# Attention values share a pair of PSUM banks with the next group's scores, transposes go in pairs, and weight rounding moves inside MLP 2's gate

## The chip, the core and the metric

One Trainium2 (trn2) chip, one of its cores. The metric is device microseconds (us) of one execution. The engines are TensorE (PE; its weight loads are listed as PEld), VectorE (DVE), ScalarE (ACT), GpSimd (POOL) and SyncE (SP, which here only issues DMA transfers). Each engine works through its own instructions in the order written; semaphores join them.

## What is computed

Local attention over chunks of 32 queries, with 8 memory keys in front of each window, then two MLPs one after the other, all in fp32 with 3072 tokens (4 x 768) of width 512 and a hidden width of 2048.

```python
for c in range(24):                       # per batch and head (8 heads of 64)
    k_full = concat([mem_k, k[c*32 - 16 : c*32 + 32 + 8]])
    scores = q_c @ k_full.T / 8
    a = exp(scores - max(scores)); a = a / (sum(a) + 1e-9)
    out[c] = a @ v_full
x = out                                   # 3072 x 512
h = x @ w1_in;  x = (h - tanh(h)) @ w1_out
h = x @ w2_in
g = h if h >= 1, 0 if h <= -1, else (h + 1)**2 / 4
out = g @ w2_out
```

The weights arrive as 64-bit floats and are rounded to fp32 on the chip.

## The kernel before

**Tiles.** A group `t` is four chunks (128 tokens) of all eight heads; there are 24 groups. A block `b` is four groups (512 tokens); there are 6. The MLPs run in 192 steps `s`: MLP 1 (`phase` 0) has 6 blocks of 16 slices `fc` of 128 hidden units, then MLP 2 (`phase` 1) the same. An fp32 product is made of three products of rounded halves: `hi*hi`, `hi*lo` and `lo*hi` (tiles `whi`, `wlo`, `xh`, `xl`, `ghi`, `glo`). So `hidden(s)` and `output(s)` are 12 matmuls of 128x512 each.

**The main loop.** Iteration `i` (called step `i` below) issues, in this order: the split of the weights of later slices (`whi` on ACT, then `wlo` on DVE), `gate_end(i)`, the split of the gate of `output(i-15)`, the events of the table `before`, `hidden(i+1)`, `gate(i+1)`, the events of the table `behind`, and `output(i-16)`. Outputs run 16 steps behind the hidden products, so block 0 of MLP 1 (steps 0 to 15) has no outputs to compute. The hidden product goes to PSUM tile `h`, of which there are two.

**The gate.** In MLP 1 it is a tanh on ACT (L371) and a subtraction on DVE (L372). In MLP 2 DVE clamps `h` (L374), ACT squares (L377), and `gate_end`, one step later, takes the larger of that and `h` on DVE (L382), which also frees `h`:

```python
gate_end(i)                 # at the start of step i: DVE, L382
...
run events "before"         # rounding of one weight slice: ACT L119, L122; DVE L128, L129, L137; L142
hidden(i + 1)
gate(i + 1)                 # DVE L374, ACT L377
```

**Rounding of weights** (`round_weights`): two ACT passes, three DVE passes and one addition (L142), on POOL for MLP 1's weights and on DVE for MLP 2's. It runs at steps 0 to 27 for MLP 1 and at steps 79 to 121 for MLP 2, one slice in most of these steps.

**Attention.** Groups 0 to 3 run ahead of the loop. The others are spread over the loop through `behind`, in four parts, one part to a step, a group to every 3.4 steps in block 0 and to every 4 later: part 0 scores (32 small fp32 matmuls on 64 rows by 32 columns of the array, 64 instructions in the trace, into two PSUM banks `s`), maximum, subtraction and exp; part 1 sum and four transposes `t`, copied to `at`; part 2 values (as many small matmuls, into two banks `v`) and normalisation `xn`; part 3 four transposes `x`, split into `xh` (ACT) and `xl` (DVE, L307), which are the next block's input. All of these take banks from one pool `ps_a` of two.

Of the kernel before, what the change touches and what calls it, by code (L numbers as in the profile page):

```python
# [55 lines left out]
ATT1 = (1, 3.4)  # L56
# [9 lines left out]
def tile_memory_attention_two_mlps(  # L66
# [24 lines left out]
    ps_a = ctx.enter_context(tc.tile_pool(name="ps_a", bufs=2, space=PSUM))  # L91
# [52 lines left out]
    def round_weights(phase, which, fc):  # L144
        round_act(phase, which, fc)
        round_mag(phase, which, fc)
        round_sign(phase, which, fc)
# [21 lines left out]
    def att_load(t):  # L169
        if t >= NG:  # L170
            return
        q = att.tile([128, NQ], F32, tag="q", name=f"q{t}")
        k = att.tile([128, NK], F32, tag="k", name=f"k{t}")
        v = att.tile([128, NV], F32, tag="v", name=f"v{t}")
        att_dma(t, q, (k[:, :NK // 2], k[:, NK // 2:]), (v[:, :NV // 2], v[:, NV // 2:]))
# [3 lines left out]
    def att_load_start(t):  # L179
# [6 lines left out]
        att_dma(t, q, (k0, k1), (v0, v1), True)  # L186

    def att_dma(t, q, k, v, weights=False):
        q = q.rearrange("p (j a c) -> p j a c", j=GC, a=NPAIR)
        k = [x.rearrange("p (j a c) -> p j a c", j=2, a=NPAIR) for x in k]  # L190
        v = [x.rearrange("p (j c) -> p j c", j=2) for x in v]
# [8 lines left out]
        if weights:  # L200
            load_weights(0, 0, t)

        for i in range(2):
# [6 lines left out]
        st[t] = {  # L210
            "q": [q[:, j] for j in range(GC)],
            "k": [k[j // 2][:, j % 2] for j in range(GC)],
            "v": [v[j // 2][:, j % 2] for j in range(GC)],
        }
# [3 lines left out]
    def att_scores(t, ps):  # L218
        qt, kt = st[t]["q"], st[t]["k"]
        sp = [ps(f"s{t}_{hh}") for hh in range(2)]  # L220
        for pr in range(NPAIR):
            for j in range(GC):
                for hh in range(2):
                    nc.tensor.matmul(  # L224
                        sp[hh][j * CHUNK:(j + 1) * CHUNK, pr * WIN:(pr + 1) * WIN],
# [6 lines left out]
    def att_exp(t):  # L232

        e = att.tile([128, 4, 2, WIN], F32, tag="e", name=f"e{t}")
        mx = att.tile([128, H], F32, tag="mx", name=f"mx{t}")
        for hh in range(2):
            s = st[t]["sp"][hh][:, :NPAIR * WIN].rearrange("p (a k) -> p a k", a=NPAIR)

            if t % GPB == 0:
                nc.vector.memset(s[:CHUNK, :, NMEM:NMEM + LEFT], NEG)  # L240
            if t % GPB == GPB - 1:
                nc.vector.memset(s[128 - CHUNK:, :, WIN - SEEN:], NEG)
            m = mx[:, hh * NPAIR:(hh + 1) * NPAIR]
            nc.vector.tensor_reduce(out=m, in_=s, op=ALU.max, axis=AX.X)
            nc.vector.tensor_tensor(  # L245
                out=e.rearrange("p (b c) u k -> p c u b k", c=2)[:, hh],
                in0=s.rearrange("p (u b) k -> p u b k", u=2),
                in1=m.rearrange("p (u b) -> p u b", u=2)[:, :, :, None].to_broadcast([128, 2, 2, WIN]),
                op=ALU.subtract,
            )  # L250
        nc.scalar.activation(out=e, in_=e, func=AF.Exp, scale=scale)  # L251
        st[t]["e"] = e
# [8 lines left out]
    def att_transpose(t, ps):  # L261
        p = ps(f"t{t}")
        e = st[t]["e"].rearrange("p g u k -> p g (u k)")
        for g in range(4):
            nc.tensor.transpose(p[:, g * GQ:(g + 1) * GQ], e[:, g, :], ident)  # L265
        at = att.tile([128, 4, GQ], F32, tag="at", name=f"at{t}")
        nc.scalar.activation(out=at, in_=p.rearrange("p (g c) -> p g c", g=4), func=AF.Copy)
        st[t]["at"] = at

    def att_values(t, ps):  # L270
        at, v = st[t]["at"], st[t]["v"]
        vp = [ps(f"v{t}_{u}") for u in range(2)]
        for g in range(4):
            for j in range(GC):
                for u in range(2):
                    nc.tensor.matmul(  # L276
                        vp[u][j * CHUNK:(j + 1) * CHUNK, g * D:(g + 1) * D],
# [6 lines left out]
    def att_norm(t):  # L284
        vp, r = st[t]["vp"], st[t]["r"]
        xn = att.tile([128, 2, 4, D], F32, tag="xn", name=f"xn{t}", bufs=1)
        for u in range(2):
            nc.vector.tensor_tensor(
                out=xn[:, u], in0=vp[u][:, :4 * D].rearrange("p (g d) -> p g d", g=4),
                in1=r[:, :, u][:, :, None].to_broadcast([128, 4, D]), op=ALU.mult,  # L290
# [296 lines left out]
```

## Time and profile before

| | us |
|---|---|
| median of 3 runs | 1192.4 (1191.47 to 1192.63) |
| the profiled execution, whole | 1190.61 |
| its span (first to last instruction) | 1188.8 |
| PE busy | 1148.5 (97%) |
| DVE busy | 788.5 (66%) |
| ACT busy | 589.0 (50%) |
| POOL busy | 42.5 (4%) |

The span runs from the first instruction to the last; the whole time holds 1.8 us more, around it. PE is busy nearly all the time, so what counts is where it is not, and how much of its busy time is small matmuls and transposes.

### The profile page before, as it was taken

Reading aid. Unit: us, or ns where it says so; the run is one execution under the profiler, and the core shown is the slowest. Engines: PE = TensorE matmul, PEld = TensorE weight load, DVE = VectorE, ACT = ScalarE, POOL = GpSimd, SP = SyncE. Lnnn points to the kernel's source line nnn. Section 1 sums busy time; section 2 is a strip of 40 time slices with the busy share of each in tenths; the row PEclk is TensorE's granted clock in tenths of the full one; section 3 lists DMA queues with packets and bytes.
Section 4 is the critical chain, followed back from the end, with each engine's and each line's share of the span. In section 5 each row is a group of like instructions: output and inputs, shape, how many; then the busy total and the mean of one; then the engine's idle time right before and its main releaser. Section 6 shows DMA issues by size and latency. Waiting matters only on the chain.

```text
span 1188.8 us, 19761 instructions
## 1 busy us (share of the span) xinstructions
PE 1148.5 (97%) x7931; PEld 923.3 (78%) x7931; DVE 788.5 (66%) x1394; ACT 589.0 (50%) x1018; POOL 42.5 (4%) x38
## 2 busy tenths in 40 slices
PE   7888999999999999999999988999999999999998
PEld 3566888888888888888887766788888888888886
DVE  5689886655655565588877777766666666665653
ACT  3456664444444454466655455454445454544443
POOL 1223221000000000000000000000000000000000
PEclk9989999999999999999999999999999999999999
DMA  9777552222221143032232122010010000000000
GB/s 230 204 200 203 150 143 63 81 60 57 81 64 45 45 107 125 2 107 107 71 107 89 55 87 89 1 71 1 1 72 1 1 36 1 1 36 1 1 36 36
DMA packets 94268, 85.18 MB, mean 72 GB/s; under 512 B 54496, under 2 KB 79072, under 8 KB 93408
## 3 DMA queue, kind: packets, MB, share of 16 engines
q1 hardware_dynamic: 94176, 83.91, 23.9%
q8 instruction: 63, 1.03, 0.4%
q14 instruction: 29, 0.24, 0.1%
HBM read 71.30 MB, written 12.58 MB: 71 GB/s over the span
## 4 chain that ended last, share of the span: by engine, by line
PE 80%; DVE 12%; ACT 3%; issue 3%; DMA 0%; SPq 0%; ACTq 0%; DVEq 0%
PE acc L407 39%; PE h L359 37%; DVE wlo L162 2%; PE v L276 2%; ACT g L377 2%; DVE g L382 2%; PE s L224 1%; DVE g L374 1%; DVE raw L137 1%; DVE glo L389 1%; ACT whi L155 1%; DVE raw L142 1%; PE t L265 1%; DVE raw L129 1%; PE x L300 1%
## 5 line engine op out<-in xcount | busy, mean ns | idle before, releaser
L162 DVE TENSOR_TENSOR wlo<-raw,whi 128x512 fp32r<-128x512 f32 x384 | 265.1, 690 | 152.4 <-ACT whi L155 152.4
L155 ACT ACTIVATE whi<-raw 128x512 fp32r<-128x512 f32 x384 | 240.0, 625 | 32.2 <-PE acc L407 31.2
L359 PE MATMUL h<-xh,whi 128*128 128x512 f32 x768 | 209.5, 395 | 14.2 <-DVE g L382 13.0
L407 PE MATMUL acc<-ghi,whi 128*128 128x512 f32 x768 | 219.0, 399 | 1.9 <-DVE y L420 1.7
L407 PE MATMUL acc<-ghi,wlo 128*128 128x512 f32 x768 | 211.8, 390 | 0.0
L407 PE MATMUL acc<-glo,whi 128*128 128x512 f32 x768 | 211.4, 389 | 0.0
L359 PE MATMUL h<-xl,whi 128*128 128x512 f32 x768 | 207.4, 392 | 1.1 <-DVE xl L307 1.1
L359 PE MATMUL h<-xh,wlo 128*128 128x512 f32 x768 | 206.8, 391 | 0.0
L377 ACT ACTIVATE g<-g,half 128x512 f32<-128x512 f32 x96 | 69.4, 723 | 265.6 <-DVE g L374 265.6
L359 PEld LDWEIGHTS h<-xh,whi 128*128 128x128 f32 x768 | 142.2, 188 | 49.8 <-ACT whi L155 19.1
L389 DVE TENSOR_TENSOR glo<-g,ghi 128x512 fp32r<-128x512 f32 x192 | 131.7, 686 | 62.4 <-PE acc L407 61.3
L359 PEld LDWEIGHTS h<-xl,whi 128*128 128x128 f32 x768 | 145.2, 189 | 32.2 <-DVE xl L307 1.6
L359 PEld LDWEIGHTS h<-xh,wlo 128*128 128x128 f32 x768 | 145.3, 189 | 30.6
L407 PEld LDWEIGHTS acc<-ghi,wlo 128*128 128x128 f32 x768 | 144.2, 188 | 31.0
L407 PEld LDWEIGHTS acc<-glo,whi 128*128 128x128 f32 x768 | 144.2, 188 | 30.6
L407 PEld LDWEIGHTS acc<-ghi,whi 128*128 128x128 f32 x768 | 139.6, 188 | 31.5 <-issue 2.1
L388 ACT ACTIVATE ghi<-g 128x512 fp32r<-128x512 f32 x192 | 119.9, 624 | 73.7 <-PE acc L407 73.6
L372 DVE TENSOR_TENSOR g<-h,g 128x512 f32<-128x512 f32 x96 | 66.2, 689 | 96.4 <-ACT g L371 96.0
L371 ACT ACTIVATE g<-h 128x512 f32<-128x512 f32 x96 | 57.2, 596 | 128.7 <-PE h L359 126.8
L374 DVE TENSOR_SCALAR g<-h 128x512 f32<-128x512 f32 x96 | 66.1, 689 | 42.8 <-PE h L359 42.6
L382 DVE TENSOR_TENSOR g<-h,g 128x512 f32<-128x512 f32 x96 | 65.7, 684 | 1.7 <-ACT g L377 1.7
L251 ACT ACTIVATE e<-e 128x512 f32<-128x512 f32 x24 | 15.2, 632 | 73.8 <-DVE e L245 73.8
(50 smaller groups left out, 599.7 us busy)
## 6 DMA issues: line engine op xcount, KB each, us to landing
stage<-w_in SPq DMA_DIRECT2D x32, 512.0 KB, 4.1
stage<-w_out SPq DMA_DIRECT2D x32, 512.0 KB, 3.4
k<-qkv_t SPq DMA_DIRECT2D x80, 128.0 KB, 4.1
v<-qkv_t SPq DMA_DIRECT2D x80, 128.0 KB, 3.2
yd<-y SPq DMA_DIRECT2D x24, 256.0 KB, 2.7
yin<-yd SPq DMA_DIRECT2D x6, 1024.0 KB, 5.5
out_t<-y SPq DMA_DIRECT2D x24, 256.0 KB, 2.1
q<-qkv_t SPq DMA_DIRECT2D x20, 256.0 KB, 3.9
```

Of the source, the lines that this page charges most:

```text
L155: nc.scalar.activation(out=hi, in_=r, func=AF.Copy)
L162: nc.vector.tensor_tensor(out=lo, in0=r, in1=hi.bitcast(F32), op=ALU.subtract)
L276: nc.tensor.matmul(vp[u][j * CHUNK:(j + 1) * CHUNK, g * D:(g + 1) * D], at[u * WIN:(u + 1) * WIN, g, j * CHUNK:(j + 1) * CHUNK], v[j][u * ...
L359: nc.tensor.matmul(hp, w[:, kc * 128:(kc + 1) * 128], x[:, kc, :], start=j == 0 and kc == 0, stop=j == 2 and kc == KC - 1,)
L371: nc.scalar.activation(out=g, in_=hp, func=AF.Tanh)
L372: nc.vector.tensor_tensor(out=g, in0=hp, in1=g, op=ALU.subtract)
L374: nc.vector.tensor_scalar(out=g, in0=hp, scalar1=-1.0, scalar2=1.0, op0=ALU.max, op1=ALU.min)
L377: nc.scalar.activation(out=g, in_=g, func=AF.Square, scale=0.5, bias=half)
L382: nc.vector.tensor_tensor(out=g_t[s], in0=hp, in1=g_t[s], op=ALU.max)
L388: nc.scalar.activation(out=hi, in_=g, func=AF.Copy)
L389: nc.vector.tensor_tensor(out=lo, in0=g, in1=hi.bitcast(F32), op=ALU.subtract)
L407: nc.tensor.matmul(acc_t[dm][:, :n], w[:, dm * 128:(dm + 1) * 128], g, start=fc == 0 and j == 0, stop=fc == FC - 1 and j == 2,)
```

## The change

- Attention of group `t` is issued in three slots: `slot_a` at step `i`, `slot_exp` at `i+1`, `slot_b` at `i+2`. Groups start every 3 steps for groups 4 to 8 and every 4 from there; group 4 starts at step 0 (before: step 1).
- `slot_a(t)` issues the values of group `t-1` and the scores of group `t` back to back. Both lie in one PSUM tile of two banks, values in the first half of each bank, scores in the second. Behind them come the normalisation of `t-1` and the maximum and subtraction of `t`. The maximum and the normalisation are one DVE instruction each (before: two).
- `slot_exp(t)` issues the exp and the sum, one step later than the maximum.
- `slot_b(t)` issues the transposes `x` of group `t-1` and `t` of group `t` back to back, into another such tile. The pool `ps_a` holds one tile of two banks, so a slot waits until the slot before it has been read.
- Keys and queries of group `t+2` are loaded at step `i+1`, values of `t+1` too; before, all of group `t+2` at part 3.
- In MLP 2 the three DVE passes and the addition of the rounding stand between the clamp and the maximum of the gate, and the maximum (`gate_end`) moves to the step of its clamp. In MLP 1 the rounding keeps its place.
- The output accumulators are two tiles of two banks (before: four of one).

```diff
-ATT1 = (1, 3.4)
+SPACE_A = (3, 4)
...
-    ps_a = ctx.enter_context(tc.tile_pool(name="ps_a", bufs=2, space=PSUM))
+    ps_a = ctx.enter_context(tc.tile_pool(name="ps_a", bufs=1, space=PSUM))
...
-    def att_scores(t, ps):
+    def att_scores(t, pair):
-        sp = [ps(f"s{t}_{hh}") for hh in range(2)]
+        sp = pair[:, :, 4 * D:].rearrange("p c (a k) -> p c a k", a=NPAIR)
...
-    def att_values(t, ps):
+    def att_values(t, pair):
-        vp = [ps(f"v{t}_{u}") for u in range(2)]
+        vp = pair[:, :, :4 * D].rearrange("p u (g d) -> p u g d", g=4)
...
+    def slot_a(t):
+        pair = ps_a.tile([128, 2, 512], F32, tag="a", name=f"a{t}")
+        if t - 1 >= PER:
+            att_values(t - 1, pair)
+        if t < NG:
+            att_scores(t, pair)
+        if t - 1 >= PER:
+            att_norm(t - 1)
+        if t < NG:
+            att_max(t)
+
+    def slot_exp(t):
+        att_exp(t)
+        att_sum(t)
+
+    def slot_b(t):
+        pair = ps_a.tile([128, 2, 512], F32, tag="a", name=f"b{t}")
+        if t - 1 >= PER:
+            att_x(t - 1, pair[:, 0, :])
+        if t < NG:
+            att_transpose(t, pair[:, 1, :])
+        if t - 1 >= PER:
+            att_xh(t - 1)
+        if t < NG:
+            att_at(t)
+        if t - 1 >= PER:
+            att_xl(t - 1)
...
-    for t in range(PER, NG):
-        b, k = t // PER - 1, t % PER
-        i = ATT1[0] + ATT1[1] * k if b == 0 else FC * b - 1 + 4 * k
-        for part in range(4):
-            at_step(behind, i + part, att_part, t, part)
-        if t + 2 < NG:
-            at_step(before, i + 3.01, att_load, t + 2)
-    at_step(before, 1.5, att_load, PER + 1)
+    for t in range(PER, NG + 1):
+        k = t - PER
+        i = SPACE_A[0] * min(k, PER) + SPACE_A[1] * max(0, k - PER)
+        at_step(behind, i, slot_a, t)
+        if t < NG:
+            at_step(behind, i + 1, slot_exp, t)
+        at_step(behind, i + 2, slot_b, t)
+        at_step(before, i + 1.01, att_load, t + 2, True, False)
+        if t - 1 >= PER:
+            at_step(before, i + 1.02, att_load, t + 1, False, True)
+    at_step(before, 0.5, att_load, PER + 1)
...
-                    at_step(before, p, round_weights, phase, w, fc)
+                    at_step(before, p, round_act, phase, w, fc)
+                    at_step(rounds, p, round_rest, phase, w, fc)
...
-        if 0 <= i < NS:
-            gate_end(i)
...
+        run(before, i)
+        second = i + 1 < NS and steps[i + 1][0] == 1
+        if not second:
+            run(rounds, i)
         if i + 1 < NS:
             hidden(i + 1)
             gate(i + 1)
+        if second:
+            run(rounds, i)
+        if i + 1 < NS:
+            gate_end(i + 1)
+        run(behind, i)
         if o >= 0:
             output(o)
```

**PE, block 1 of MLP 1.** The order of PE's instructions around groups 8 and 9 before the change. `h17` is the hidden product of step 17, `acc` the output accumulators, `v8`, `t8` and `x8` the values and transposes of group 8; the 32 matmuls of the values alternate between `v8_0` and `v8_1`.

```order
L265 MATMUL t8_1689<-ident_99,e8_1641 128x128 x4
L407 MATMUL acc0_0_1696<-ghi0_1574,whi1_0_1578 128x512
...
L359 MATMUL h18_1733<-xh_0_1_943,wlo0_18_1650 128x512 x4
L276 MATMUL v8_0_1749<-v8_1313,at8_1694 32x64
L276 MATMUL v8_1_1750<-v8_1313,at8_1694 32x64
...
L359 MATMUL h19_1831<-xh_0_1_943,wlo0_19_1714 128x512 x4
L300 MATMUL x8_1849<-ident_99,xn8_1783 128x128 x4
L407 MATMUL acc0_0_1696<-ghi2_1716,whi1_2_1720 128x512
```

The same place after the change; `a9` and `b9` are the shared tiles of the slots of group 9.

```order
L385 MATMUL h17_1638<-xh_0_1_1006,wlo0_17_1582 128x512 x4
L287 MATMUL a9_1654<-v8_1319,at8_1577 32x64 x32
L231 MATMUL a9_1654<-k9_1313,q9_1312 32x64 x32
L434 MATMUL acc0_0_1726<-ghi0_1584,whi1_0_1588 128x512 x2
...
L385 MATMUL h19_1827<-xh_0_1_1006,wlo0_19_1742 128x512 x4
L307 MATMUL b9_1843<-ident_99,xn8_1719 128x128 x4
L273 MATMUL b9_1843<-ident_99,e9_1721 128x128 x4
L434 MATMUL acc0_0_1726<-ghi2_1744,whi1_2_1748 128x512 x2
```

Four interruptions of the large matmuls for each group have become two.

**ACT, block 0.** ACT's order around the exp of group 5 before: `g5` is the tanh of step 5, `e5` the exp, `whi0_7` the split of a weight slice.

```order
L371 ACTIVATE g5_940<-h5_927 128x512
L302 ACTIVATE xh_0_1_943<-x4_945 128x4x128
L251 ACTIVATE e5_986<-e5_986 128x512
L155 ACTIVATE whi0_7_995<-raw00_7_840 128x512
L119 ACTIVATE raw00_9_999<-stage00_9_807 128x512
```

And after, from the step of the group's maximum on:

```order
L397 ACTIVATE g4_846<-h4_833 128x512
L154 ACTIVATE whi0_6_922<-raw00_6_788 128x512
L119 ACTIVATE raw00_8_926<-stage00_8_750 128x512
L122 ACTIVATE stage00_8_750<-stage00_8_750 128x512
L397 ACTIVATE g5_960<-h5_947 128x512
L261 ACTIVATE e5_916<-e5_916 128x512
L154 ACTIVATE whi0_7_968<-raw00_7_824 128x512
```

The subtraction that the exp needs is issued on DVE right behind `g4`'s, so a whole step of ACT's work now stands between the two.

**DVE, MLP 2.** DVE's order around the gate of step 112 before: `raw11_8` is the weight slice that is rounded, `y95` the copy of a finished output.

```order
L389 TENSOR_TENSOR glo96_7572<-g96_6820,ghi96_7571 128x512
L162 TENSOR_TENSOR wlo1_96_7577<-raw11_0_7050,whi1_96_7575 128x512
L128 TENSOR_SCALAR raw11_8_7581<-raw11_8_7581 128x512
L129 TENSOR_SCALAR raw11_8_7581<-raw11_8_7581 128x512
L137 SCALAR_TENSOR_TENSOR raw11_8_7581<-stage11_8_7438,raw11_8_7581 128x512
L142 ISA raw11_8_7581<-stage11_8_7438,raw11_8_7581 128x1024
L374 TENSOR_SCALAR g112_7601<-h112_7588 128x512
L420 COPY y95_7616<-acc0_80_6874 128x512
L420 COPY y95_7616<-acc2_80_6876 128x512
L162 TENSOR_TENSOR wlo0_114_7628<-raw10_2_6129,whi0_114_7626 128x512
L382 TENSOR_TENSOR g112_7601<-h112_7588,g112_7601 128x512
```

After:

```order
L400 TENSOR_SCALAR g112_7439<-h112_7426 128x512
L128 TENSOR_SCALAR raw11_8_7423<-raw11_8_7423 128x512
L129 TENSOR_SCALAR raw11_8_7423<-raw11_8_7423 128x512
L137 SCALAR_TENSOR_TENSOR raw11_8_7423<-stage11_8_7280,raw11_8_7423 128x512
L142 ISA raw11_8_7423<-stage11_8_7280,raw11_8_7423 128x1024
L408 TENSOR_TENSOR g112_7439<-h112_7426,g112_7439 128x512
L447 COPY y95_7459<-acc0_80_6719 128x512
L447 COPY y95_7459<-acc1_80_6720 128x512
L161 TENSOR_TENSOR wlo0_114_7471<-raw10_2_5973,whi0_114_7469 128x512
```

The clamp has moved ahead of the four rounding passes, and the maximum ahead of the next step's `wlo`.

## Rows read from the trace of the kernel before

**Rows 1.** The page's first line

```profile
span 1188.8 us, 19761 instructions
```

**Rows 2.** Stretches: from:to and length, PE, PEld, DVE, ACT, POOL busy (instructions); clock, DMA share, GB/s

```profile
0.00:42.73 42.73, 31.08 (x604) 16.31 (x604) 22.38 (x58) 14.59 (x24) 5.00 (x10) 0.92 0.94 237
...
46.41:114.00 67.59, 58.52 (x726) 43.78 (x724) 58.33 (x121) 42.06 (x77) 19.33 (x15) 0.95 0.69 190
...
118.41:508.75 390.34, 390.34 (x3631) 315.73 (x3626) 246.55 (x466) 189.68 (x332) 16.29 (x13) 1.00 0.28 78
...
595.00:800.00 205.00, 189.90 (x819) 152.06 (x818) 153.85 (x259) 105.96 (x187) 0.00 (x0) 1.00 0.20 68
```

**Rows 3.** DVE's waits in block 0, 46.45 to 114.00: us, times, longest

```profile
DVE wlo L162 <- ACT whi L155: 4.9, 4, 1.3
...
DVE s L242 <- PE s L224: 1.3, 1, 1.3
DVE s L240 <- PE s L224: 1.0, 1, 1.0
```

**Rows 4.** ACT's waits in block 0, 42.8 to 118.3

```profile
ACT e L251 <- DVE e L245: 17.2, 4, 5.7
```

**Rows 5.** DVE's groups in block 0, 46.45 to 114.00: busy, mean ns, idle before

```profile
L245 DVE TENSOR_TENSOR e<-s,mx 128x256 f32<-128x256 f32 x8 | 3.4, 425 | 0.3
L244 DVE TENSOR_REDUCE mx<-s 128x4 f32<-128x256 f32 x8 | 3.4, 420 | 0.1
...
L256 DVE TENSOR_REDUCE r<-e 128x8 f32<-128x512 f32 x4 | 2.7, 675 | 0.0
L257 DVE TENSOR_SCALAR r<-r 128x8 f32<-128x8 f32 x4 | 0.9, 232 | 0.1
L258 DVE RECIPROCAL r<-r 128x8 f32<-128x8 f32 x4 | 0.8, 203 | 0.1
```

**Rows 6.** PE's waits in block 0, 42.8 to 118.3

```profile
PE s L224 <- DVE xl L307: 4.4, 2, 2.8
```

**Rows 7.** Timeline of PE around one group's scores: start, length, instruction

```profile
137.90 1.07 PE L359 MATMUL h<-xl,whi 128*128 128x512 f32 x4
138.81 1.07 PE L359 MATMUL h<-xh,wlo 128*128 128x512 f32 x4
139.81 0.86 PE L224 MATMUL s<-k,q 64*32 64x64 f32 x64
...
141.62 0.62 PE L407 MATMUL acc<-ghi,wlo 128*128 128x512 f32 x2
```

**Rows 8.** The same scores as far as they had started at 140.00

```profile
139.81 0.41 PE L224 MATMUL s<-k,q 64*32 64x64 f32 x25
```

**Rows 9.** Timeline of PE around one group's transposes x

```profile
132.87 1.07 PE L359 MATMUL h<-xh,wlo 128*128 128x512 f32 x4
133.78 0.60 PE L300 MATMUL x<-ident,xn 128*128 128x128 f32 x4
...
135.16 0.62 PE L407 MATMUL acc<-ghi,wlo 128*128 128x512 f32 x2
```

**Rows 10.** Timeline of PE: the values of group 0, ahead of the loop

```profile
11.31 1.50 PE L276 MATMUL v<-start,at 64*32 64x64 f32 x64 [0.26 <-ACT at L267]
```

**Rows 11.** Waits of PE and of DVE in MLP 2's start, 595 to 800

```profile
PE h L359 <- DVE g L382: 13.0, 12, 1.7
...
DVE wlo L162 <- ACT whi L155: 44.6, 33, 1.4
```

**Rows 12.** Timeline of DVE, one step of MLP 2 with rounding

```profile
712.48 0.68 DVE L374 TENSOR_SCALAR g<-h 128x512 f32<-128x512 f32 x1
714.54 0.69 DVE L162 TENSOR_TENSOR wlo<-raw,whi 128x512 fp32r<-128x512 f32 x1 [1.38 <-ACT whi L155]
...
717.56 0.42 DVE L128 TENSOR_SCALAR raw<-raw 128x512 f32<-128x512 f32 x1
...
719.91 0.68 DVE L374 TENSOR_SCALAR g<-h 128x512 f32<-128x512 f32 x1
```

More of the change, by code (lines that the diff above doesn't have):

```diff
@@ L167, in tile_memory_attention_two_mlps, with att_load @@
     NQ, NK, NV = GC * NPAIR * CHUNK, GC * NPAIR * WIN, GC * 4 * D
-    def att_load(t):
+    def att_load(t, keys=True, values=True):
         if t >= NG:
             return
[L172 to L175, printed above, removed]
+        if keys:
+            q = att.tile([128, NQ], F32, tag="q", name=f"q{t}")
+            k = att.tile([128, NK], F32, tag="k", name=f"k{t}")
+            att_keys(t, q, (k[:, :NK // 2], k[:, NK // 2:]))
+        if values:
+            v = att.tile([128, NV], F32, tag="v", name=f"v{t}")
+            att_v(t, (v[:, :NV // 2], v[:, NV // 2:]))
     free = []
@@ L199, in att_dma, with att_v @@
             nc.sync.dma_start(out=k[j // 2][:, j % 2], in_=ks[j, :, :, :WIN])
-        if weights:
-            load_weights(0, 0, t)
+        st[t] = {
+            "q": [q[:, j] for j in range(GC)],
+            "k": [k[j // 2][:, j % 2] for j in range(GC)],
+        }
+    def att_v(t, v):
+        v = [x.rearrange("p (j c) -> p j c", j=2) for x in v]
+        src = qkv[t * GC:(t + 1) * GC]
         for i in range(2):
@@ L396, in output @@
         whi, wlo = split_t.pop((s, 1))
-        for dm in range(KC):
-            if fc == 0:
-                acc_t[dm] = ps_acc.tile([128, 512], F32, tag=f"acc{dm}", name=f"acc{dm}_{s}")
+        if fc == 0:
+            for i in range(2):
+                pair = ps_acc.tile([128, 2, 512], F32, tag=f"acc{i}", name=f"acc{i}_{s}")
+                acc_t[2 * i], acc_t[2 * i + 1] = pair[:, 0, :], pair[:, 1, :]
         products = [(j, dm) for j in range(3) for dm in range(KC)]
@@ L424, in output @@
                     nc.sync.dma_start(out=out[dm * 128:(dm + 1) * 128, b * N:(b + 1) * N], in_=y)
-    def ps_plain(name):
-        return ps_a.tile([128, 512], F32, tag="a", name=name)
-    before, behind = {}, {}
+    before, rounds, behind = {}, {}, {}
     def at_step(events, i, f, *args):
@@ L517, in tile_memory_attention_two_mlps, with run @@
     att_xl(PER - 1)
+    def run(events, i):
+        for _, f, args in sorted(events.pop(i, []), key=lambda e: e[0]):
+            f(*args)
     for i in range(-1, NS + LAG):
@@ L533, in tile_memory_attention_two_mlps @@
             gate(i + 1)
-        for _, f, args in sorted(behind.pop(i, []), key=lambda e: e[0]):
-            f(*args)
+        if second:
[3 more added lines that the diff above has]
+        run(behind, i)
         if o >= 0:
             output(o)
-    assert not before and not behind
+    assert not before and not rounds and not behind
 def _windows(np, mem, x):
```

108 lines of the change are left out of this document (44 added, 64 removed).

## The prediction

> **What bounds the kernel now.** I read the page first: the span is 1188.8 us [rows 1], and the whole profiled execution 1190.6, so 1.8 us lie around the span. Then I cut the span into stretches [rows 2] and looked where PE is not busy. There are three kinds of stretch that the change touches.
>
> Block 0 of MLP 1, 46.41 to 114.00 (from DVE's first gate in the loop to the last `xl` that block 1 needs): PE is busy 58.5 of 67.6 us, DVE 58.3. Both are near full, yet neither is full: they wait for each other. DVE waits for `whi` on ACT four times, 4.9 us, and twice for scores, 1.3 and 1.0 us [rows 3]. The first has its cause one engine on: ACT waits 17.2 us at four exps [rows 4], in order, with `whi` behind them. So DVE makes the subtraction, ACT starts the exp only then, then `whi`, and DVE stands still until that. The second comes from PE, which waited 4.4 us for `xl` before two groups' scores [rows 6], since the scores need both attention banks.
>
> Blocks 1 to 5, 118.41 to 508.75: PE is busy all 390.3 us [rows 2]. No engine but PE matters there; time can only come from what PE executes.
>
> The start of MLP 2, 595 to 800: PE is busy 189.9 of 205 us [rows 2]. Of the missing 15.1 us, 13.0 are hidden products that wait for L382, the maximum that frees `h` [rows 11]. DVE in turn waits 44.6 us there for `whi`, at 33 steps [rows 11]. One step shows why [rows 12]: after the clamp DVE stands 1.38 us until ACT has squared and split, and only then come `wlo`, the maximum and, at the end, the rounding and the next clamp: 719.91 - 712.48 = 7.43 us, where 12 + 12 matmuls of 128x512 take 24 x 0.2275 = 5.46 us (0.91 for four [rows 7]).
>
> **The change, part by part.** *MLP 2's gate.* It adds no instruction. The four rounding passes (719.91 - 717.56 = 2.35 us [rows 12]) now stand between clamp and maximum, while ACT squares; the square and `whi` are done before they end, so the 1.38 us go. The step of rows 12 becomes 7.43 - 1.38 = 6.05 us, and 5.45 in one without the extra `xl`. That is PE's own pace. Summed over the stretch: DVE is busy 153.9 us, and in the steps without rounding (15 of the 33: the table of steps puts 18 slices there) the maximum now waits for the square in order, at most the 1.38 that `wlo` waits today: 153.9 + 20.7 = 175 us against PE's 189.9. So DVE is no bound on the average; where rounding and an `xl` meet, it falls 0.6 us behind, for which two `h` tiles leave room. What is queued behind the maximum is the next step's `wlo`, whose product comes last of hidden's three. I count 0.8 us of the 15.1 as left: **-14.3 us**. In all later steps DVE waits for the square too, at no cost: PE was the bound there with 1.38 us of idle DVE in every step. If none of the idle DVE time came back, PE would keep its 15.1.
>
> *Block 0.* The exp moves one step behind the subtraction, so ACT no longer stands before `whi`: 4.9 us of DVE's waits go. Scores no longer wait for `xl` of the part that was issued just ahead of them, since a hidden product (2.73 us) lies between `slot_b` and the next `slot_a`, and the longest such wait was 2.8 us [rows 6]: 2.3 us go. The two maxima of 420 ns become one reduction of 512 columns; the sum is one of that size, at 675 ns [rows 5]: 4 x (0.84 - 0.675) = 0.7 us go. Against this, scores and sum of group 8 now come before the last `xl` (steps 12 and 13): 0.675 + 2 x 0.425 + 0.675 + 0.23 + 0.20 = 2.6 us more [rows 5]. So 67.6 - 4.9 - 2.3 - 0.7 + 2.6 = 62.3 us: **-5.3 us**. DVE is then busy nearly throughout, and PE follows it. SP's queue changes with it: keys of a group are asked for up to two steps earlier, ahead of a weight slice or two; the stretch moved 190 GB/s at a share of 0.69, the same bytes in 62.3 us are 206, and ahead of the loop the transfers reached 237 at 0.94 [rows 2]. So they fit, with less room than before; if the cover were gone, block 0 would keep its length.
>
> Ahead of the loop only the last group's chain counts, with one reduction less: **-0.2 us**.
>
> *Blocks 1 to 5.* Scores cost [rows 7] 141.62 - 138.81 - 2 x 0.91 = 0.99 us: the time from the hidden group before them to the second group after them, less that of two groups. The last of the 64 starts 0.86 - 0.22 = 0.64 us after the first (0.22 is the length of one), so 0.35 us is entering and leaving. Values have the same form, and I give them the same price. Transposes cost 135.16 - 132.87 - 1.82 = 0.47 us a set [rows 9]. A group is 2 x 0.99 + 2 x 0.47 = 2.92 us of PE.
>
> After the change entering and leaving is paid once: 0.35 + 0.64 + 64 x r, where r is the spacing of the second 64. The trace has no run of 128. In the first 0.19 us 25 had started, 7.6 ns apart [rows 8]; the other 39 take 0.45 us, 11.5 ns apart. I take 11.5, since it is what the run settles to: 1.73 us, 0.25 less than two. The ends are 7.6 (0.50 less) and the slowest 64 of the trace, (1.50 - 0.22) / 63 = 20 ns [rows 10] (0.29 more). Of eight transposes in a row only the entry is saved; three spacings of the four take 0.60 - 0.28 = 0.32, so eight take 0.47 + 4 x 0.107 = 0.90 against 0.94. Per group 0.29 us, for the 15 groups that are paired with a next: 4.4. Scores and transposes of group 8 have left this stretch, 0.99 + 0.47 = 1.5, for block 0, where PE has time. **-5.9 us**, between -9.6 and +2.3.
>
> [...]
>
> Accumulators in pairs: the first output of a block waits for two copies, one on each engine, and not for one; the hidden product between (2.73 us) covers both, of 0.7 us at most. Nothing, and up to 0.7 at each of 11 block ends if DVE is late.
>
> **Sum.** 1190.6 - 0.2 - 5.3 - 5.9 - 14.3 = 1164.9 us on the profiled execution's scale. The median of the three runs is 1.8 us above that; with part of it, **1165.5 us**.
>
> **Rivals.** (a) *The second 64 run slowly.* PE has its instructions queued when a run begins, which is what the fast first 25 suggest; a run twice as long may live on what arrives. At 20 ns blocks 1 to 5 lose 2.3 instead of gaining 5.9: 1174. For it: the slowing within one run [rows 8]. Against: the slow run [rows 10] fell in a stretch without a queue of large matmuls ahead. [...]
> (b) *MLP 2 keeps half its stall*, because the four copies, the `xl`s and the rounding meet on DVE at the same steps and the maximum, now behind the rounding, frees `h` 2.35 us later after its clamp than it would alone. 1165.5 + 7 = 1172.5. Against: 175 us in 190. Chance 0.10.
> (c) *Block 0 is not shortened*: loads or the handover of the single attention tile take the place of the exp. 1165.5 + 5.3 = 1171. Chance 0.12. It also has a better side: if DVE's other idle time there (67.6 - 58.3 - 7.2 = 2.1 us) goes too, and the second 64 run at 7.6 ns, 1160: chance 0.13.
> (d) *Slower: the single attention tile.* Every slot waits for the readers of the slot before. If `xl` leaves DVE later than one hidden product after its transposes, PE stands before each of the 20 `slot_a`s. At the 2.8 us of rows 6 that is 56 us: 1165.5 + 56 = 1221. It decides at 27 / 20 = 1.3 us a slot, that is at an `xl` 4 us late. Against: from block 1 on two whole steps lie between slots, and the PE waits of 4.4 us were with nothing between. Chance 0.03.
> (e) *The waits only change their names* and the kernel stays within 0.2% (2.4 us, about what this measurement can tell from no change): 0.01.
>
> **How the numbers follow.** The forecast itself, 1162 to 1169, has 0.51, (a) 0.10, (b) 0.10, (c) 0.12, its better side 0.13. 1158 to 1174 holds the forecast, the better side, (b), (c) and half of (a), above 0.8. Faster 0.96, same 0.01, slower 0.03.
>
> **What would show it.** Right: in 595 to 780 PE's wait for the maximum is gone and DVE's wait for `whi` has become a shorter one for the square, in steps without rounding alone; in block 0 ACT's waits before exps fall from 17.2 us to little and DVE is busy over 90%; a slot of values and scores takes 1.7 us of PE between large matmuls. Wrong: PE waits at `slot_a` for `xl`; the 64 scores behind the values stand further apart than the values; DVE waits for weights in block 0; the time between two groups in blocks 1 to 5 falls by less than 0.1 us.

## The result, and the profile after

The changed kernel takes 1154.3 us (1151.12 to 1157.31, 4 runs) against 1192.2 us (1191.47 to 1192.63, 4 runs): a ratio of 0.968, 95% interval 0.966 to 0.971. It is faster, by 38 us where 27 were forecast, and below the range of 1158 to 1174. The profiled execution takes 1154.25 us.

Where the time came from shows best if one reads, in PE's timeline of both traces, when the hidden product of a step starts (us from the start of the span):

| from hidden product of step | before | after | length before | after | change | predicted |
|---|---|---|---|---|---|---|
| start of the span to 0 | 0 | 0 | 42.73 | 40.34 | -2.4 | -0.2 |
| 0 to 17 (block 0) | 42.73 | 40.34 | 75.68 | 67.71 | -8.0 | -5.3 |
| 17 to 80 (blocks 1 to 5) | 118.41 | 108.05 | 390.18 | 382.78 | -7.4 | -5.9 |
| 80 to 98 | 508.59 | 490.83 | 97.92 | 97.97 | 0.0 | 0 |
| 98 to 128 (start of MLP 2) | 606.51 | 588.80 | 183.00 | 163.26 | -19.7 | -14.3 |
| 128 to 191 | 789.51 | 752.06 | 342.72 | 342.72 | 0.0 | 0 |
| 191 to the end | 1132.23 | 1094.78 | 56.60 | 57.53 | +0.9 | 0 |

Every forecast gain came, and each was larger than forecast; only the end, forecast at nothing, became longer. Three stretches repeat within 0.3 us in all traces of the same code: 80 to 98, 98 to 128 and 128 to 191. The others do not. Among the runs further below, block 0 took 73.8 and 73.9 us in two that have attention as before (e1, e11), and 66.4 to 67.9 in six that have it as changed (e0, e2, e3, e4, e6, e12); blocks 1 to 5 took 391.8 and 391.9, against 382.7 to 383.5. So block 0 gained 5.9 to 9.3 us, depending on the traces compared, and blocks 1 to 5 gained 6.7 to 9.1. Part of block 0's spread is the granted clock of TensorE. It is 0.93 of full speed there before and 0.97 after, and 1.00 in the traces with 66.4 and 66.5 us; in the changed kernel's trace it stands at 0.50 from 104.3 to 107.7, which begins inside PE's wait of 1.9 us for the block's last `xl`.

The stretches of the changed kernel (the columns are those of [rows 2]; the second is block 0 as the prediction bounded it, first gate to last `xl`):

```profile
span 1152.3 us, 19690 instructions
```

```profile
0.00:40.34 40.34, 28.83 (x595) 15.72 (x604) 21.30 (x49) 14.69 (x24) 5.85 (x10) 0.96 0.94 229
...
44.03:104.69 60.66, 54.19 (x794) 43.22 (x792) 58.87 (x117) 44.13 (x79) 19.33 (x15) 1.00 0.91 245
...
108.05:490.83 382.78, 382.78 (x3622) 315.92 (x3620) 242.79 (x424) 192.82 (x331) 17.06 (x13) 1.00 0.28 77
...
588.80:752.06 163.26, 163.26 (x722) 135.16 (x720) 139.12 (x235) 97.83 (x169) 0.00 (x0) 1.00 0.22 72
```

In block 0 DVE is now busy 97% of the time (58.87 of 60.66 us; 58.3 of 67.6 in [rows 2]). From step 98 to 128, the start of MLP 2, PE has no idle time left. All that PE still waits for, from the first hidden product to the end, is this:

```profile
PE a L287 <- DVE xl L318: 3.9, 3, 1.3
PE h L385 <- DVE xl L318: 1.9, 1, 1.9
PE h L385 <- ACT xh L313: 0.9, 2, 0.7
PE acc L434 <- ACT y L445: 0.6, 1, 0.6
```

The first is the slot waiting for the readers of the shared tile. The prediction had named it as a sign of being wrong (rival d); it came 3 times, all in block 0, where DVE and not PE sets the pace. DVE's wait from 44 to 105 and ACT's for the exps from 42 to 105 answer to [rows 3, 4]: ACT's exps have come down from 17.2 us to 0.2, and DVE's only wait is the one in front of its first gate; the waits for `whi` are gone.

```profile
DVE g L398 <- ACT g L397: 3.0, 1, 3.0
```

```profile
ACT e L261 <- DVE e L251: 0.2, 1, 0.2
```

Waits in MLP 2, 577 to 785, answer to [rows 11]: PE has none. DVE's 44.6 us for `whi` have become short waits for the square, and DVE now waits 14.7 us for PE's hidden products (0.8 us before, in 595 to 800):

```profile
DVE g L408 <- ACT g L403: 16.2, 19, 0.9
DVE g L400 <- PE h L385: 14.7, 14, 1.4
...
DVE wlo L161 <- ACT whi L154: 3.6, 3, 1.2
```

DVE's timeline there, a step with rounding and one without (answers to [rows 12]). From clamp to clamp a step with rounding takes 696.33 - 690.97 = 5.36 us, without any wait; in the step without rounding the maximum waits 0.85 us for the square, as forecast:

```profile
690.97 0.68 DVE L400 TENSOR_SCALAR g<-h 128x512 f32<-128x512 f32 x1
691.57 0.42 DVE L128 TENSOR_SCALAR raw<-raw 128x512 f32<-128x512 f32 x1
...
693.92 0.68 DVE L408 TENSOR_TENSOR g<-h,g 128x512 f32<-128x512 f32 x1
...
696.33 0.68 DVE L400 TENSOR_SCALAR g<-h 128x512 f32<-128x512 f32 x1
697.86 0.69 DVE L408 TENSOR_TENSOR g<-h,g 128x512 f32<-128x512 f32 x1 [0.85 <-ACT g L403]
```

PE's timeline around a pair of transposes and around a slot of values and scores (answers to [rows 7, 9]):

```profile
86.84 1.08 PE L385 MATMUL h<-xh,wlo 128*128 128x512 f32 x4
87.75 0.60 PE L307 MATMUL b<-ident,xn 128*128 128x128 f32 x4
88.19 0.60 PE L273 MATMUL b<-ident,e 128*128 128x128 f32 x4
88.55 1.17 PE L385 MATMUL h<-xh,whi 128*128 128x512 f32 x4
89.56 1.08 PE L385 MATMUL h<-xl,whi 128*128 128x512 f32 x4
...
109.90 1.07 PE L385 MATMUL h<-xh,wlo 128*128 128x512 f32 x4
110.90 0.80 PE L287 MATMUL a<-v,at 64*32 64x64 f32 x60
...
111.56 0.82 PE L231 MATMUL a<-k,q 64*32 64x64 f32 x62
112.31 1.19 PE L434 MATMUL acc<-ghi,whi 128*128 128x512 f32 x4
113.34 1.08 PE L434 MATMUL acc<-ghi,wlo 128*128 128x512 f32 x4
```

The transposes cost 89.56 - 86.84 - 2 x 0.91 = 0.90 us, as forecast. The slot costs 113.34 - 109.90 - 2 x 0.91 = 1.62 us, where 1.73 were forecast and two runs had cost 1.98. By the prediction's own form, 0.35 + 0.64 + 64 x r, r is 9.8 ns: the second 64 run as fast as the first, whose 63 spacings take 0.64 us. The slot's 128 matmuls, on 64 rows by 32 columns of the array, start within 1.4 us (110.90 to 112.31), 11 ns apart on average.

### The profile page after: what moved, and what is told of

Same layout as the page of the kernel before. It is cut to its first block, busy times and chain, and to the rows that moved or that the text cites. A ratio compares the mean times of both kernels' runs of the same rounds, so it can differ in the third digit from the quotient of the medians.

```text
span 1152.3 us, 19690 instructions
## 1 busy us (share of the span) xinstructions
PE 1129.2 (98%) x7923; PEld 923.1 (80%) x7931; DVE 786.8 (68%) x1338; ACT 596.0 (52%) x1018; POOL 42.5 (4%) x38
## 3 DMA queue, kind: packets, MB, share of 16 engines
q8 instruction: 63, 1.03, 0.4%
## 4 chain that ended last, share of the span: by engine, by line
PE 93%; DVE 3%; DMA 2%; SPq 1%; issue 0%; ACT 0%; DVEq 0%
PE acc L434 46%; PE h L385 43%; PE a L287 1%; DMA start<-qkv_t 1%; PE a L231 1%; PE b L307 1%; DVE wlo L161 1%; DVE g L398 1%; PE b L273 1%; DMA stage<-w_in 1%; DMA starty<-qkv_t 1%; SPq L202 1%; DVE raw L129 0%; DVE raw L137 0%; DVE raw L128 0%
## 5 line engine op out<-in xcount | busy, mean ns | idle before, releaser
L434 PE MATMUL acc<-ghi,whi 128*128 128x512 f32 x768 | 215.2, 394 | 0.7 <-ACT y L445 0.6
L385 PE MATMUL h<-xh,whi 128*128 128x512 f32 x768 | 206.5, 391 | 1.0 <-ACT xh L313 0.9
L142 POOL TENSOR_TENSOR raw<-raw,stage 128x512 int32<-128x512 int32 x32 | 41.8, 1305 | 137.1 <-DVE raw L137 103.9
```

What stands on the lines that cost most here:

```text
L142: eng.tensor_tensor(out=bits, in0=bits, in1=stage[:, :, 0], op=ALU.add)
L385: nc.tensor.matmul(hp, w[:, kc * 128:(kc + 1) * 128], x[:, kc, :], start=j == 0 and kc == 0, stop=j == 2 and kc == KC - 1,)
L434: nc.tensor.matmul(acc_t[dm][:, :n], w[:, dm * 128:(dm + 1) * 128], g, start=fc == 0 and j == 0, stop=fc == FC - 1 and j == 2,)
```

## The experiments

**Either half alone.** e1 is the kernel before with the gate's new order; e2 is the changed kernel with the gate and the rounding as before. The core of e1's edit, which e2 undoes:

```diff
-        if 0 <= i < NS:
-            gate_end(i)
...
+        second = i + 1 < NS and steps[i + 1][0] == 1
+        if not second:
+            run(rounds, i)
         if i + 1 < NS:
             hidden(i + 1)
             gate(i + 1)
+        if second:
+            run(rounds, i)
+        if i + 1 < NS:
+            gate_end(i + 1)
```

> The kernel before with the change's MLP 2 part alone (rounding between clamp and maximum, maximum in the step of its clamp); attention as before. Theory A, the stall was larger than PE's idle time in the profile: 30 steps from step 98 on took 183.0 us before and 30 x 5.44 = 163.3 at PE's pace, so 19.7 us go and the kernel takes 1172.5 us. Rival B, only PE's 15.1 us of idle time are to be had in MLP 2 and the other 4.6 us of its gain came with the attention part: 1177 us. Under both the attention stretches stay as before.

> The changed kernel with MLP 2's gate and rounding as before. Theory A: the stall of MLP 2 is back in full (steps 98 to 128 again 183 us), the rest stays: 1154.3 + 19.7 = 1174 us. Rival B (part of MLP 2's gain came with attention): 1169 us. Ahead of the loop: if the 2.4 us by which the first hidden product came earlier in the changed kernel belong to its new order there, it starts near 40.3 us here; if they are chance of the loads, it lies anywhere between 39 and 43.

e1 takes 1173.8 us against 1190.6 (0.986, 0.983 to 0.988), e2 1172.0 us (0.985, 0.982 to 0.988). Steps 98 to 128 take 163.2 us in e1 and 183.7 in e2. So the gate alone gives MLP 2's whole gain and the attention alone the rest. The two savings, 16.9 and 18.6 us, add up to 35.5; e3 below, timed beside them, saves 36.8.

**Which edit of the gate.** e3 puts the maximum back into the next step and leaves the rounding behind the clamp; e4 leaves the maximum early and puts the rounding back ahead of the hidden product.

```diff
e3
+        if 0 <= i < NS:
+            gate_end(i)
...
-        if i + 1 < NS:
-            gate_end(i + 1)
e4
-        second = i + 1 < NS and steps[i + 1][0] == 1
-        if not second:
-            run(rounds, i)
+        run(rounds, i)
```

> The changed kernel with the maximum back in the next step, behind wlo; the rounding stays behind the clamp. Theory A, the rounding as cover for ACT's square and split is what counts: 1154 us, PE without waits in MLP 2. Rival B, the earlier release of h counts: 1154 plus up to 15 us, with PE waiting for the maximum again.

> The changed kernel with the rounding back ahead of the hidden product; the maximum stays in its clamp's step and so waits for the square in every step (0.85 us in the changed kernel's steps without rounding). Theory A: a step with rounding takes DVE 5.45 + 0.85 = 6.3 us against PE's 5.44, so over the 16 rounding steps of 22 (steps 100 to 121) DVE needs about 128 us against 120, and some 8 us of the 19.7 come back: 1162 us. Rival B (the early maximum alone is enough): 1154 us.

e3: 1153.9 us (0.969, 0.967 to 0.972), the same as the changed kernel, 163.2 us for the 30 steps. e4: 1160.0 us (0.974, 0.971 to 0.977), 171.9 us for them; PE waits there again:

```profile
PE acc L434 <- ACT y L445: 3.8, 1, 3.8
PE h L385 <- DVE g L408: 1.3, 3, 0.6
```

These are 5.1 of the 8.7 us more. 3.8 of them are one stall at the end of a block: DVE reaches its copies of the accumulators late, and ACT's copies wait for them. Behind it, from 675.0 to 681.8, the granted clock is 0.50, so that the stretch has 0.98, where the changed kernel has 1.00:

```profile
586.15:758.07 171.92, 166.80 (x721) 136.60 (x720) 138.94 (x235) 96.44 (x169) 0.00 (x0) 0.98 0.20 68
```

So moving the rounding does the work by itself. With it in place, the step of the maximum makes no difference that these runs show; the early maximum alone brings 11 of the 19.7 us. What e4 loses falls mostly at one block's end, where the paired accumulators take part; how much of it four accumulators would leave was not run.

**The exp a step later.** e5 issues the exp in the step of its subtraction, as before (`att_exp(t)` moves from `slot_exp` to the end of `slot_a`).

> The changed kernel with the exp in the step of its maximum, as before the change; the sum stays a step later. Theory A, ACT standing at the exp with whi behind it is what held DVE up in block 0: DVE waits about 1.25 us for whi at each of 5 groups again, block 0 is 5 to 6 us longer, 1160 us. Rival B, the handover of the attention banks was the cause: 1154 us, DVE as busy as in the changed kernel (59 of 61 us).

1160.0 us (0.975, 0.972 to 0.978). Hidden products 0 to 17 take 73.9 us instead of 67.7 (66.4 to 67.9). The old chain is back: ACT waits for the subtraction, DVE for `whi`, PE for `whi` too. PE's list has 3.7 us of stalls without a releaser besides; of these DVE, which sets the pace, waited for 0.7 us (at `xn`). So the cost of the exp's place is best read from DVE's 6.1 us.

```profile
ACT e L261 <- DVE e L251: 23.0, 5, 5.7
```

```profile
DVE wlo L161 <- ACT whi L154: 6.1, 5, 1.3
```

```profile
PE h L385 <- ACT whi L154: 4.0, 3, 2.0
```

**Paired or apart.** From block 1 on, e7 and e8 issue scores and transposes `t` behind the output product, values and `x` ahead of it. In e7 all that reads the tile (normalisation, maximum, `xh`, `at`, `xl`) also moves behind the output. In e8 normalisation, `xh` and `xl` stay right behind values and `x`:

```diff
+    def late_b(t):
+        pair = pairs.pop(("b", t))
         if t < NG:
             att_transpose(t, pair[:, 1, :])
-        if t - 1 >= PER:
-            att_xh(t - 1)
-        if t < NG:
             att_at(t)
...
         if o >= 0:
             output(o)
+        run(late, i)
```

> The changed kernel with the scores of a group behind the step's output and no longer right behind the values, and the transposes t behind the output and no longer right behind x, from block 1 on; tiles, steps and all other work as changed. Theory A: what blocks 1 to 5 gained is the entering and leaving of the small matmuls, paid once in place of twice, 0.40 us a group: 16 groups, 6 us more, 1160 us. Rival B: it comes from elsewhere (less waiting, other banks): 1154 us.

> The changed kernel, but from block 1 on the scores of a group stand behind the output product and the values of the group before ahead of it, and so the transposes t and x; this time normalisation, the split xh and xl of the group before stay where they were, right behind their own values and transposes. So nothing but entering and leaving the small matmuls is doubled. Theory A (a merged slot saves the 0.35 us of entering and leaving and no more, and the rest of e7 was the late xh): by e7's own rows two runs cost 1.01 + 1.00 and two sets of transposes 0.47 + 0.47, 2.95 us a group against 2.52; 15 groups, 6.5 us more than the changed kernel, about 1160.5 us; steps 17 to 80 take 389 us, and PE does not wait for xh from block 1 on beyond what the changed kernel has. Rival B (two excursions to one tile cost a wait on each other, wherever xh stands): near e7's 1163.1, steps 17 to 80 near 394 us. Rival C (the pairing is worth nothing by itself): within 2 us of the changed kernel.

e7: 1163.1 us (0.977, 0.975 to 0.979). e8: 1183.0 us (0.992, 0.990 to 0.995), which no theory had expected. Its loss lies in block 0 and at the start of block 1: there nothing stands between the two halves of a slot but the moved readers. PE's waits, 38 to 133:

```profile
PE a L231 <- DVE xn L297: 11.0, 5, 4.3
PE b L273 <- DVE xl L318: 10.9, 4, 2.9
```

Scores write the second half of each bank and `xn` reads the first, yet in this order the scores wait for `xn`: the wait does not go by the half. (Both halves lie in the same banks, so this does not tell whether it goes by the bank or by the tile.) In the changed kernel both matmul runs are issued ahead of any reader; hidden 0 to 17 take 67.7 us there and 80.6 in e8. Later the product between the halves covers it (no PE wait from 169 to 516), and there e8 answers the question. Steps 24 to 80 take 345.4 us against 339.5 to 339.9 in the changed kernel's traces, 5.5 to 5.9 us for the 13 pairs of slots that they hold, 0.42 to 0.45 us a pair, where the rows gave 2.95 - 2.52 = 0.43. In e7, above its theory A's 1160, the same steps take 349.2; there PE waits for `xh` at three block ends, 2.1 us by the list.

**Accumulators.** e6 has four accumulators of one bank again.

```diff
-            for i in range(2):
-                pair = ps_acc.tile([128, 2, 512], F32, tag=f"acc{i}", name=f"acc{i}_{s}")
-                acc_t[2 * i], acc_t[2 * i + 1] = pair[:, 0, :], pair[:, 1, :]
+            for dm in range(KC):
+                acc_t[dm] = ps_acc.tile([128, 512], F32, tag=f"acc{dm}", name=f"acc{dm}_{s}")
```

> The changed kernel with four accumulators of one bank, as before the change (the groups ahead of the loop then all use the attention tile). Theory A: the copies of two accumulators of one tile wait for each other, which costs 0.7 us at the very end and 0.6 us at one block's end: 1153 us, last copy 0.43 us after the last matmul's start and not 1.15. Rival B: the pairs cost nothing and the later end is chance: 1154.3.

> The changed kernel once more, on this chip. If the 6 us between its runs (1151.1 to 1157.3) come from stretches at the lower clock ahead of the loop and in block 0 and from the loads there, the spread is here too, the first hidden product starts anywhere from 38 to 43 us, and everything from step 17 on takes the same time within 0.5 us. If they do not, the spread lies in the loop.

e6: 1150.4 us (1149.31 to 1150.85; 0.966, 0.964 to 0.968), the fastest of all that leave nothing out; the changed kernel beside it (e0) 1152.8 (0.968, 0.966 to 0.971). In e0 the first hidden product starts at 39.3, and from step 17 on all takes the time of the first trace within 0.4 us, so what differs between the two traces lies ahead of it; e0's four runs span 1.5 us, where the first four spanned 6.2. From hidden product 191 on, e6 takes 55.9 us against 57.5. Its other gain, 1.3 us from hidden 0 to 17 (66.5 against e0's 67.8), goes with the granted clock of 1.00 against 0.97 and can't be laid to the accumulators. The last copy by ACT in the changed kernel, and then in e6: in a pair, ACT's copy waits for DVE's of the other bank; with four tiles it waits for PE alone. So here the wait goes by the tile, for these are two banks. The last matmuls start at 1147.49 and 1144.48, so the last copy follows by 1.15 us and by 0.42; 0.7 of the 1.6 us lie here. The rest lies at the block's end before, where the changed kernel's PE waits 0.6 us by the list.

```profile
1148.64 0.60 ACT L445 ACTIVATE y<-acc 128x512 f32<-128x512 f32 x1 [0.76 <-DVE y L447]
```

```profile
1144.90 0.60 ACT L444 ACTIVATE y<-acc 128x512 f32<-128x512 f32 x1 [0.76 <-PE acc L433]
```

**What bounds block 0 now.** e9 gives six of block 0's splits `wlo` to GpSimd (e10 does so on e6); e14 leaves out one DVE pass of the rounding, L129.

```diff
e9, e10
-        nc.vector.tensor_tensor(out=lo, in0=r, in1=hi.bitcast(F32), op=ALU.subtract)
+        eng = nc.gpsimd if which == 0 and 4 <= s <= 14 and s % 2 == 0 else nc.vector
+        eng.tensor_tensor(out=lo, in0=r, in1=hi.bitcast(F32), op=ALU.subtract)
```

> The changed kernel, with the split wlo of six weight slices of block 0 (steps 4, 6, 8, 10, 12, 14) on GpSimd and not on VectorE. Theory A (in block 0 VectorE is now what bounds: busy 59.2 of 61.0 us, with TensorE busy 54.5): six splits of 0.76 us leave VectorE, 4.6 us, and hidden 0 to hidden 17 fall from 67.7 to about 63.5 us; the kernel gains about 4, near 1150. Rival B (the handover between slots or the loads bound block 0): no change of more than 1 us. Rival C (GpSimd, which has the additions of the rounding at 1.3 us each, delivers wlo late): TensorE waits for wlo, and block 0 is longer than now.

> The kernel with four output accumulators of one bank each, and the six splits of block 0 on GpSimd as well. If both gains are what they seem, they add up: four accumulators gave 2.4 us in the first comparison, and the splits what the kernel beside this one shows; by theory A about 1146.5 us. If the splits give nothing or cost time, 1150 or more.

> The changed kernel without the second of the three VectorE passes of the rounding (the one that shifts and masks) in MLP 1's loop: part of the computation is left out, so that VectorE has 15 instructions of 0.427 us less in block 0, 6.4 us, and nothing else changes on other engines. Theory A (VectorE's time bounds block 0): hidden 0 to hidden 17 fall by 4 to 6 us from 67.7, until TensorE's own work bounds (54.5 of 61.0 us busy), and the kernel by as much, to about 1149. Rival B (the handover between slots and gates bounds it, and VectorE is only busy because it follows): less than 2 us.

e9: 1152.9 us (0.967, 0.965 to 0.969), hidden 0 to 17 66.7 us; e10: 1154.4 (0.968, 0.966 to 0.970). No gain, and theory A's expectation missed: the traces of the changed code with the same granted clock of 1.00 take 66.4 and 66.5. (e10 is 4 us above e6 alone; PE stands 2.6 us in its block 0 without a releaser, and its granted clock is 0.96 from 40 to 118, so that pair tells nothing more.) Yet e14 takes 1146.3 us (0.963, 0.961 to 0.964) with hidden 0 to 17 in 61.4 us, 5.0 less than 66.4 at the same clock, for 6.4 us of DVE's passes left out: DVE's time does bound block 0. Why e9 didn't lower it is in its DVE groups, 44 to 105 (first the changed kernel, then e9): the splits went, and the two rounding passes became longer by 4.2 us in all.

```profile
L161 DVE TENSOR_TENSOR wlo<-raw,whi 128x512 fp32r<-128x512 f32 x16 | 12.2, 764 | 0.0
...
L129 DVE TENSOR_SCALAR raw<-raw 128x512 int32<-128x512 int32 x15 | 6.4, 427 | 0.5
L128 DVE TENSOR_SCALAR raw<-raw 128x512 f32<-128x512 f32 x15 | 6.3, 418 | 0.0
```

```profile
L128 DVE TENSOR_SCALAR raw<-raw 128x512 f32<-128x512 f32 x15 | 8.6, 571 | 0.0
L129 DVE TENSOR_SCALAR raw<-raw 128x512 int32<-128x512 int32 x15 | 8.3, 556 | 0.5
L162 DVE TENSOR_TENSOR wlo<-raw,whi 128x512 fp32r<-128x512 f32 x10 | 7.9, 785 | 0.0
```

What grew are single instructions of the two short passes, and only those that met one of GpSimd's six splits. Of the 30 passes, 23 stay at 0.41 to 0.43 us, three take 0.47 to 0.62, and four take 1.34 to 1.39. The first of these four began 0.22 us behind GpSimd's split and ended 0.28 us behind it:

```profile
51.53 1.28 POOL L162 TENSOR_TENSOR wlo<-raw,whi 128x512 fp32r<-128x512 f32 x1
```

```profile
51.75 1.34 DVE L128 TENSOR_SCALAR raw<-raw 128x512 f32<-128x512 f32 x1
```

DVE's own splits meet GpSimd as well: five of the 16 in the changed kernel run beside an addition of the rounding (L142) and take 0.85 to 1.47 us, the others 0.65 to 0.68. How GpSimd holds VectorE up, no trace here shows.

**The start.** PE stands inside scores with no releaser named, that is without anything in the trace that it waited for: twice in the kernel before, 4.1 us, and three times in e1, which has the same start, 7.2 us. e11 and e12 put small matmuls ahead of everything, in the kernel before and in the changed one:

```diff
+    for _ in range(66):
+        nc.tensor.matmul(warm_ps[:, :16], zeros[:, :128], zeros[:, :16], start=True, stop=True)
     warm(WARM)
```

> The kernel before, with 66 matmuls of 16 columns on zeros put ahead of everything on TensorE, where it waits for the first loads anyway. They compute nothing that is used; they move every later instruction of TensorE 132 places back in its stream (a matmul and its weight load are two). In the kernel before TensorE stood without a releaser at its 705th and its 961st instruction, 256 apart, both inside scores. Theory A (the stream arrives in pieces of 256 instructions, and a piece comes late while the transfers are full): the stalls stay at those counts and so leave the scores: they now fall in the values of groups 1 and 2, near the 50th and the 25th of the 64, and the scores of groups 2 and 3 run without a stall that has no releaser. The time may go either way by some us. Rival B (loads of keys come late, and the profile doesn't show the wait): the stalls stay in the scores, after 40 of 64 in group 2 and after 18 of 64 in group 3.

> The changed kernel with the same 66 matmuls ahead. Its stall without a releaser stood at its 447th instruction, after 62 of 64 scores of group 1. Theory A: it moves 132 instructions on in the program's order, that is ahead of those scores, to the end of group 0's transposes x, and any other such stall falls in values. Rival B: it stays after 62 of 64 scores of group 1. First hidden product within 2 us of 40 by either.

e11: 1186.1 us against 1191.5 (0.996, 0.994 to 0.997), a small gain by adding instructions; its first hidden product starts at 39.03 instead of 42.73. The stalls have left the scores (rival B falls) but do not turn up in the values, as theory A had it: they are gone. e12: 1153.5 us (0.969, 0.967 to 0.970), first hidden product at 38.84; no such stall ahead of it either. PE's scores of the start in the kernel before, then in e1 (its third stall, 1.54 us, stands ahead of these):

```profile
22.64 0.66 PE L224 MATMUL s<-start,start 64*32 64x64 f32 x40
24.71 0.43 PE L224 MATMUL s<-start,start 64*32 64x64 f32 x24 [1.42 <-issue]
...
31.63 0.41 PE L224 MATMUL s<-starty,start 64*32 64x64 f32 x18
34.71 0.70 PE L224 MATMUL s<-starty,start 64*32 64x64 f32 x46 [2.68 <-issue]
```

```profile
23.46 0.66 PE L223 MATMUL s<-start,start 64*32 64x64 f32 x40
26.05 0.43 PE L223 MATMUL s<-start,start 64*32 64x64 f32 x24 [1.93 <-issue]
...
32.97 0.41 PE L223 MATMUL s<-starty,start 64*32 64x64 f32 x18
37.14 0.94 PE L223 MATMUL s<-starty,start 64*32 64x64 f32 x46 [3.77 <-issue]
```

They stand behind the same instruction in both, and 256 instructions of PE (matmuls, weight loads and four waits) lie between the two stalls of the kernel before; e1 has 254 records there, since two matmuls between are without one. And ahead of the end of each, a packet passes on a DMA queue of its own, here in the kernel before between 31.75 and 32.00 (packets, MB, share):

```profile
q8 instruction: 1, 0.02, 29.5%
```

PE goes on 2.4 to 3.0 us behind it, as it does behind those that begin after 22.0 (kernel before), 23.25 and 34.5 (e1). I read these as late pieces of PE's program, while the transfers are full (share 0.94 in [rows 2]). The packets agree in number: the page of the kernel before has 63 of that queue, 1.03 MB in all, for PE's 7931 matmuls and 7931 weight loads, so 252 of these to a packet (an estimate, since no trace shows what a packet holds), and 252 lie between the two stalls, besides the four waits.

The traces of all runs bear this reading out. They hold 27 such stalls of 0.7 us or more; e0, e3 and e11 have none. Counted in PE's records from the 447th, where most have their first, every one stands within 6 of a multiple of 256, and PE goes on 2.3 to 2.9 us behind the start of a packet of that queue (once 3.7). In e12, whose program has 132 more instructions ahead, one such stall does turn up, later and in a place of another kind: at the 2241st record, 7 x 256 + 2 behind the 447th, inside a hidden product.

```profile
72.06 0.62 PE L385 MATMUL h<-xh,wlo 128*128 128x512 f32 x2 [1.16 <-issue]
```

So the place goes by the count of instructions, as theory A had it, and not by the scores.

## Why the prediction was right or wrong

The sum took 25.7 us off, and 36.5 went from the span: 5.4 us more in MLP 2, 2.7 in block 0, 2.2 ahead of the loop and 1.5 in blocks 1 to 5, less 0.9 at the end. That is why the time lies below the range. The mechanisms of the three large parts were right; their sizes were too small, and two terms were put at almost nothing.

**MLP 2: mechanism right, size wrong.** The step that failed is "-14.3 us", of PE's idle 15.1: what the stall cost was 19.7. Idle time taken from busy rows understates a stall: a matmul counts as busy 0.39 us in the timeline, though the next starts 0.227 us behind it, so up to 0.16 us of each gap in front of PE passes as work. The count was in [rows 2] all along: 819 matmuls x 0.2275 = 186.3 of 205 us, 18.7 lost and not 15.1. Steps 98 to 128 of the kernel before hold 15.1 us of idle PE as well, and were shortened by 19.7, to 30 x 5.44 us. The idle time lies in 17 gaps, so 17 x 0.16 = 2.7 of the other 4.6 us are of that kind. Another 1.2 us stand behind 15 of the gaps, where the second matmul starts 0.31 us behind the first; the rest is scattered.

```profile
606.51:789.51 183.00, 167.90 (x721) 133.83 (x720) 137.92 (x233) 94.92 (x168) 0.00 (x0) 1.00 0.18 61
```

The 0.8 us that the prediction left did not stay. Rival (b) fell. By e3 it is the place of the rounding, and not that of the maximum, that carries this.

**Block 0: right, undersized.** First gate to last `xl`: -6.9 (67.59 to 60.66) against -5.3. The sum had 62.3 us, with DVE busy 60.2 and 2.1 idle; measured are 58.87 and 1.8. The terms that were mis-sized are DVE's. Group 8's two subtractions were put at 0.85 us more, but ten take 3.8 us where eight took 3.4, since a pair behind a joined maximum overlaps (0.76 us for both). The joined normalisation was left out (3.0 us before, 2.7 after), and `wlo` has come down from 12.5 to 12.2 us. That is 1.0 of the 1.3 us of busy time. Another 1.1 us lie behind the last `xl` (118.41 - 114.00 = 4.41 before, 3.36 after), where the scores of group 8 had stood; the prediction had counted these under blocks 1 to 5. e5 shows that the exp's place carries 6.1 us of DVE's time, e14 that DVE now bounds the block. Rival (c) fell, and with 1.8 us of DVE's idle time left its better side did not come either. That PE then follows DVE and that the loads fit (245 GB/s at 0.91) was right.

**Blocks 1 to 5.** 11.5 ns for the second 64 should have been 9.8: a group saves 0.40 us (0.36 and 0.04 for the transposes, whose 0.90 was right), not 0.29. Fifteen groups give 6.0, and the transposes `t` of group 8 another 0.5; 6.5 of the 7.4. The lengths of the steps give more. A step without attention takes 5.44 us. Before, one with scores or values takes 6.45 and one with transposes 5.93, 3.00 us a group; after, they take 7.09 and 6.35, 2.56. So a group saves 0.44, fifteen 6.6, and with group 8's transposes 7.1 of the 7.4 are found. What is left is less than the 1.7 us by which the traces with attention as before differ here. Rivals (a) and (d) fell; of (d) there are the 3.9 us of waits in block 0.

**Ahead of the loop.** -0.2 failed: the prediction priced only DVE's instructions there, and passed over 4.1 us of stall without a releaser. e11 shows that the loop could start 3.7 us earlier with 66 matmuls put in front, which move all that follows on in PE's program; its first scores start at 7.55 us there and not at 5.41. In the profiles of the new start these stalls take nothing (e0, e3) to 3.7 us (e2), and the first hidden product starts between 37.8 and 40.5, not in the order of the stalls. So how much of the 2.4 us belongs to the new order is open, and so is what makes a piece late in one start and not in another: nothing here set the order of instruction pieces against loads.

**Accumulator pairs.** "Nothing" failed at the end of the kernel, where no hidden product is left as cover: e6 gives 1.6 us there. The table shows only 0.9, since the span ends 3.7 us behind the start of the last copy in the changed kernel and in e6, and 4.4 in the kernel before; no run shows why.

## What to carry to other kernels

Size a stall on TensorE by instructions times pace, not by its idle time (15.1 us idle from step 98 to 128, 19.7 gained). Put work that can wait into the gap where its engine would stand still for another engine (the rounding alone, e3: 163.2 us for these steps and not 183.0), and issue all writers of a shared tile ahead of its readers (hidden 0 to 17: 67.7 us, and 80.6 in e8). Before moving VectorE work to GpSimd, look for short VectorE passes that would run at the same time (0.42 us became up to 1.39 in e9). Before laying a few us to a change, look at the granted clock of the stretch and at other traces of the same code (block 0 as changed took 66.4 to 67.9 us).

## What was not expected of the hardware

Six splits on GpSimd held up the VectorE passes that met them: a pass of 0.42 us then took 1.34 to 1.39, and the 4.3 us taken from VectorE came back as 4.2. A start of 66 useless matmuls made the kernel before 5.5 us faster (3.7 of them ahead of the loop, with both stalls of its start gone). All 27 of PE's stalls of 0.7 us or more without a releaser, in scores and in a hidden product alike, stood within 6 of a multiple of 256 records of PE, 2.3 to 3.7 us behind a packet of 0.02 MB on a queue of its own.
